# Loading weight pieces three items ahead, and splitting the rounding from the subtraction

## The chip, the cores and the metric

The kernel runs on one core of a Trainium2 chip. The metric is the device time of one execution in microseconds (us), from three runs. The engines are named as the profile names them: PE multiplies matrices, ACT is the scalar engine, DVE the vector engine, POOL the GpSimd engine, and SP issues most of the transfers. Each works through its own instructions in order and waits for the others by semaphores.

## The reference

An attention is followed by two feed-forward layers, and all data are float32.

```python
scores = q @ k.T / 8 + bias          # 4 batches x 8 heads, 576 x 576, D = 64
x = softmax(scores) @ v              # -> 2304 tokens x 512
h = x @ w_in                         # 512 -> 2048
x = (h * clip(h + 3, 0, 6) / 6) @ w_out
e = argmax(x @ w_gate)               # 8 experts, one for each token
out = gate * relu(x @ w1[e]) @ w2[e]
```

The change touches the conversion of `w_in` and `w_out` alone. They come as 64-bit floats, in 32 pieces of 128 x 512 numbers.

## The kernel before

**Attention.** The work is cut into 80 items (a chunk of rows, a unit of four heads, a pair of heads). In the loop over `s`, one pass does the scores of item `s`, the exponentials and sums of item `s-1`, the transposes of item `s-3` and the product with V of item `s-4`. The string `ORDER = "T0 S T1 X0 X1 Q0 Q1 P N"` sets the order within a pass: `S` is the place of the side work, between the two halves of the transposes (T0, T1). A transposed half is copied out of PSUM by ACT and by DVE.

**Side work.** `Moe.early` hangs steps on passes. Pieces 0 to 3 of the weights are converted there, in passes from 36 on, eight passes apart. The load brings the piece as pairs of 32-bit words into the tile `wraw` (512 KB, issued on SP). Then follow `s_a` (ACT, scales the upper word, L611), `s_b` (DVE, shift, L614), `s_c` (DVE, two steps, L617 and L618: the float32 value is then in `t[1]`), and `s_d`: ACT rounds that to the high part (L621) and DVE subtracts the high part from the value and gets the low part (L622). The last two belong to one step.

**First feed-forward layer.** It works in blocks of 256 tokens. A unit is one block and 128 of the 2048 inner features: `l1_` has 12 matmuls with 256 columns (L679), ACT adds and cuts (`r`, L685), DVE makes `t` (L686), ACT the high part of `g` (L688), DVE the low part (L691); `l2_`, three units behind, has 6 matmuls with 512 columns (L709). The first three blocks run interleaved over 48 units, numbered `g` = 0 to 47 here. Pieces 4 to 31 are converted meanwhile: `tick(p)` gives four functions, of which `l1_` calls the first after `t`, the second and third after the high `g`; the fourth comes after the low `g`. Two of three units have a tick: 28 in all.

The results of L679 go to four PSUM banks in turn. When the third block's accumulators are made, in `l2_` with `b == 2`, they take two of the four for good, so from there a result of L679 has two banks, each free again when DVE has made its `t`.

Of the kernel before, what the change touches and what calls it, by code (L numbers as in the profile page):

```python
# [6 lines left out]
F32 = mybir.dt.float32  # L7
# [4 lines left out]
ALU = mybir.AluOpType  # L12
# [3 lines left out]
B, H, S, D = 4, 8, 576, 64  # L16
# [502 lines left out]
class Moe(Base):  # L519
# [83 lines left out]
    def w_steps(self, p, t):  # L603

        nc = self.nc
        raw = self.raws.pop(p)
        w = self.pieces[p] = self.w_piece(p)
        a, b = t[0], t[1].bitcast(I32)

        def s_a():  # L610
            nc.scalar.activation(a, raw[:, :, 1].bitcast(F32), AF.Copy, scale=2.0 ** -112)  # L611

        def s_b():
            nc.vector.tensor_scalar(b, a.bitcast(I32), 3, None, op0=ALU.logical_shift_left)  # L614

        def s_c():
            nc.vector.scalar_tensor_tensor(b, raw[:, :, 0], 29, b, op0=ALU.logical_shift_right, op1=ALU.bitwise_or)  # L617
            nc.vector.scalar_tensor_tensor(b, a.bitcast(I32), -2147483648, b, op0=ALU.bitwise_and, op1=ALU.bitwise_or)  # L618

        def s_d(lo):  # L620
            nc.scalar.copy(w[:, 0:512], t[1])  # L621
            lo.tensor_tensor(w[:, 512:], t[1], w[:, 0:512].bitcast(F32), op=ALU.subtract)  # L622

        return s_a, s_b, s_c, s_d

    def w_early(self, p):

        nc = self.nc
        S = {}

        def load():
            self.w_load(p, "cv" if p % 2 else "V2")

        def first():
            t = [self.tl("bt0", [512], name="cva"), self.tl("bt1", [512], name="cvb")]
            S["f"] = self.w_steps(p, t)
            S["f"][0]()

        return [load, first, lambda: S["f"][1](), lambda: S["f"][2](), lambda: S["f"][3](nc.vector)]


    def x_load(self, b):
# [518 lines left out]
            self.conv[p][2]()  # L1161
            self.w_loads(p + (3 if p < 6 else 4))

    def w_d(self, p):
        self.conv.pop(p)[3](self.nc.vector)

    def tick(self, p):
        return (lambda: self.w_b(p + 1), lambda: self.w_d(p), lambda: self.w_a(p + 2), lambda: self.w_c(p + 1)) if p < 32 else ()

    def early(self, N):  # L1170

        ex = {}
        add = lambda s, f: ex.setdefault(s, []).append(f)
        self.loaded, self.conv = 4, {}
        add(31, self.setup)
        add(34, self.setup2)
        for p in range(4):
            for k, f in enumerate(self.w_early(p)):
                add(36 + 8 * p + k, f)
        gen = self.emit()  # L1180
        self.first = gen
        add(73, lambda: [self.x_load(b) for b in range(3)])
        add(N - 3, lambda: self.w_loads(6))
        add(N - 1, lambda: self.w_a(4))
        add(N, lambda: (self.x_prep(0), self.w_b(4)))
        add(N + 1, lambda: (self.w_c(4), next(gen)))
        add(N + 2, lambda: (self.x_prep(1), next(gen)))
        return ex
# [200 lines left out]
```

## Time and profile before

| what | value |
|---|---|
| median of 3 runs | 1071.23 us (1069.64 to 1074.22) |
| profiled execution, its own time | 1073.36 us |
| its span, first to last instruction | 1071.6 us |
| attention passes with side work of this kind | about 209 to 311 us of the span |
| 48 interleaved units | about 360 to 511 us of the span |

The profiled execution has its time 1.8 us above its span, and stands 2.1 us above the median. An engine's busy share says little here; what counts is, stage by stage, which wait PE sees.

### The profile page before, as it was taken

To read this page: it belongs to the slowest core of one execution; us is meant where nothing else is said; L and a number is where in the kernel's file an instruction comes from. 1 tells how busy PE (TensorE), PEld (TensorE's weight loads), DVE (VectorE), ACT (ScalarE), POOL (GpSimd) and SP (SyncE) were. 2 spreads that over 40 slices of the span, in tenths; PEclk is the share of its full clock that TensorE was granted. 3 is DMA by queue.
4 is the path that set the end of the run, shared out by engine and by line. 5 is a ranking of instruction groups with operands and counts; after the bars stand their busy time and mean duration, and the time that the engine had idled before them with its cause. 6 is when DMAs were issued, how large, how long until landed. Compare 5 with 4: busy or idle time off the path is not lost. (4 is left out here: it accounts for less than half of the span.)

```text
span 1071.6 us, 22490 instructions
## 1 busy us (share of the span) xinstructions
PE 1014.0 (95%) x8373; PEld 799.7 (75%) x8373; DVE 620.8 (58%) x1578; ACT 539.5 (50%) x1222; POOL 220.6 (21%) x273
## 2 busy tenths in 40 slices
PE   5898999989999989999999999999999989999996
PEld 2355556767777779988888889888887868777774
DVE  4886886768887767775445343436464633355310
ACT  4677788767778745554333333333352233354421
POOL 0132233534454200000010000002212242221111
PEclk9999999989999989999999999999999989999998
DMA  7564582423234134440202011010502185786850
GB/s 243 177 195 154 176 270 75 116 75 100 78 101 119 58 120 128 127 135 3 72 9 40 1 40 41 1 40 1 201 17 50 53 272 189 270 288 259 329 171 32
DMA packets 62198, 129.29 MB, mean 121 GB/s; under 512 B 13820, under 2 KB 35708, under 8 KB 59264
## 3 DMA queue, kind: packets, MB, share of 16 engines
q1 hardware_dynamic: 57424, 117.69, 33.3%
q0 software_dynamic: 4512, 9.49, 3.0%
q8 instruction: 68, 1.11, 0.4%
q10 hardware_dynamic: 144, 0.59, 0.2%
q14 instruction: 50, 0.41, 0.1%
HBM read 164.08 MB, written 14.65 MB: 167 GB/s over the span
## 5 line engine op out<-in xcount | busy, mean ns | idle before, releaser
L709 PE MATMUL acc<-wp,g 128*128 128x512 f32 x864 | 225.3, 396 | 0.7 <-DVE t L686 0.6
L679 PE MATMUL ph<-xh,wp 128*128 128x256 f32 x1024 | 207.0, 285 | 2.5 <-DVE eT L368 1.3
L679 PEld LDWEIGHTS ph<-xh,wp 128*128 128x128 f32 x1024 | 166.3, 189 | 12.2 <-issue 3.9
L709 PEld LDWEIGHTS acc<-wp,g 128*128 128x128 f32 x864 | 153.1, 189 | 27.5 <-DVE t L686 1.2
L344 POOL TENSOR_SCALAR e<-e,st 128x576 f32<-128x576 f32 (+1 forms) x160 | 126.2, 800 | 229.5 <-DVE st L342 109.2
L679 PE MATMUL ph<-xl,wp 128*128 128x256 f32 x512 | 144.2, 282 | 0.4 <-issue 0.4
L327 DVE CUSTOM_DVE_ANT_0 e<-sc,bias 128x576 f32<-128x576 f32 (+1 forms) x160 | 116.0, 752 | 46.4 <-PE sc L324 42.6
L685 ACT ACTIVATE r<-ph,small 128x256 f32<-128x256 f32 x144 | 67.5, 468 | 124.1 <-PE ph L679 119.0
L335 ACT ACTIVATE e<-e,st 128x576 f32<-128x576 f32 (+1 forms) x160 | 123.0, 774 | 0.0
L686 DVE SCALAR_TENSOR_TENSOR t<-r,ph 128x256 f32<-128x256 f32 x144 | 60.3, 419 | 107.8 <-ACT r L685 98.8
L688 ACT ACTIVATE g<-t 128x256 fp32r<-128x256 f32 x144 | 60.2, 418 | 114.2 <-DVE t L686 113.2
L1032 PE MATMUL peh<-ws,xt 128*128 128x512 f32 x408 | 102.8, 406 | 4.1 <-PEq L1341 4.0
L324 PE MATMUL sc<-K,q 64*128 64x288 f32 (+1 forms) x640 | 104.6, 426 | 0.4 <-DVE st L327 0.4
L679 PEld LDWEIGHTS ph<-xl,wp 128*128 128x128 f32 x512 | 96.7, 189 | 3.4
L783 POOL DMA_INDIRECT tab_d<-small x18 | 18.2, 1009 | 380.1 <-DVE small L781 343.0
L691 DVE SCALAR_TENSOR_TENSOR g<-t,g 128x256 fp32r<-128x256 f32 x144 | 61.0, 424 | 56.2 <-ACT g L688 55.7
L1032 PEld LDWEIGHTS peh<-ws,xt 128*128 128x128 f32 x408 | 76.9, 192 | 22.2 <-issue 4.9
L378 PE MATMUL po<-eT,V 128*64 128x128 f32 (+1 forms) x1280 | 82.2, 271 | 4.2 <-ACT eT L366 2.4
L1060 PE MATMUL peo<-ws,ehh 128*128 128x512 f32 x272 | 86.2, 398 | 0.0
L362 PEld LDWEIGHTS pt<-cst,e 64*128 64x128 f32 x1296 | 60.3, 139 | 34.5 <-issue 10.4
L378 PEld LDWEIGHTS po<-eT,V 128*64 128x64 f32 x1280 | 64.3, 138 | 27.4 <-issue 14.7
L362 PE MATMUL pt<-cst,e 64*128 64x64 f32 x1296 | 72.6, 232 | 8.6 <-ACT eT L366 3.5
(215 smaller groups left out, 1453.4 us busy)
## 6 DMA issues: line engine op xcount, KB each, us to landing
er<-in_we SPq DMA_DIRECT2D x46, 1024.0 KB
er<-in_we SPq DMA_DIRECT2D x86, 512.0 KB
xb<-in_xb SPq DMA_DIRECT2D x38, 512.0 KB
wraw<-in_wf SPq DMA_DIRECT2D x32, 512.0 KB
cv<-in_xb SPq DMA_DIRECT2D x11, 512.0 KB
K<-in_kT SPq DMA_DIRECT2D x8, 576.0 KB
xr<-xT_d SPq DMA_DIRECT2D x9, 512.0 KB
y_d<-y SPq DMA_DIRECT2D x18, 256.0 KB
```

Source lines behind the costliest of these rows:

```text
L324: nc.tensor.matmul(self.sc[i][:R, n, :288], q[d, pr, :], self.kv[u][d, pr, n * 288:(n + 1) * 288], start=True, stop=True, tile_position=(6 ...
L327: nc.vector.tensor_tensor_reduce(out=e[:R, j, :].rearrange("p (n s) -> p n s", n=2), in0=self.sc[j][:R, :, :288], in1=self.bias[c][:R, 4 * ...
L335: self.nc.scalar.activation(e[:R, j, :], e[:R, j, :], AF.Exp, scale=-1.0, bias=st[:R, j:j + 1], accum_out=st[:R, 4 + j:5 + j])
L344: nc.gpsimd.tensor_scalar(e[:R, j, :], e[:R, j, :], st[:R, 6 + j:7 + j], 1.0, op0=ALU.mult, op1=ALU.mult)
L362: nc.tensor.transpose(pts[h][:, i - a, :], src[i][d], self.ident[d, d], tile_position=(64 * h, 0))
L378: nc.tensor.matmul(po[64 * j:64 * j + 64, :], vm[:, 2 * pr + j, kb, :], eT[:, 2 * kb + j, :], start=kb == 0, stop=False, tile_position=(0, ...
L679: nc.tensor.matmul(ph, w, x[c], start=n == 0, stop=n == 11)
L685: nc.scalar.activation(r, ph, AF.Relu, bias=self.three)
L691: nc.vector.scalar_tensor_tensor(g[:, 1], t, 1.0 / 6.0, g[:, 0].bitcast(F32), op0=ALU.mult, op1=ALU.subtract)
L709: nc.tensor.matmul(acc[t], x, w, start=f == 0 and i == 0, stop=f == 15 and i == 2)
L1032: nc.tensor.matmul(ph[:, n, :], a, w, start=c == 0 and i == 0, stop=c == 3 and i == 2)
L1060: nc.tensor.matmul(d["po"], a, w, start=f == 0 and i == 0, stop=f == 7 and i == 2)
```

## The change

The step `s_d` becomes two, `s_d` (ACT's rounding) and `s_e` (DVE's subtraction). In the attention a piece is loaded at pass 34 + 8p instead of 36 + 8p, `s_a` stays at 37 + 8p, `s_b` at 38 + 8p, `s_c` at 39 + 8p, the rounding at 40 + 8p, and the subtraction goes to 41 + 8p. In a tick the rounding moves ahead of the shift of the next piece, into the first of the four functions; the subtraction stays in the second.

```diff
-        def s_d(lo):
+        def s_d():
             nc.scalar.copy(w[:, 0:512], t[1])
-            lo.tensor_tensor(w[:, 512:], t[1], w[:, 0:512].bitcast(F32), op=ALU.subtract)
-
-        return s_a, s_b, s_c, s_d
+
+        def s_e():
+            nc.vector.tensor_tensor(w[:, 512:], t[1], w[:, 0:512].bitcast(F32), op=ALU.subtract)
+
+        return s_a, s_b, s_c, s_d, s_e
...
-        return [load, first, lambda: S["f"][1](), lambda: S["f"][2](), lambda: S["f"][3](nc.vector)]
+        return [load, first] + [lambda k=k: S["f"][k]() for k in range(1, 5)]
...
-    def w_d(self, p):
-        self.conv.pop(p)[3](self.nc.vector)
-
     def tick(self, p):
-        return (lambda: self.w_b(p + 1), lambda: self.w_d(p), lambda: self.w_a(p + 2), lambda: self.w_c(p + 1)) if p < 32 else ()
+
+        return (lambda: (self.conv[p][3](), self.w_b(p + 1)), lambda: self.conv.pop(p)[4](), lambda: self.w_a(p + 2),
+                lambda: self.w_c(p + 1)) if p < 32 else ()
...
         for p in range(4):
-            for k, f in enumerate(self.w_early(p)):
-                add(36 + 8 * p + k, f)
+            for k, f in zip((34, 37, 38, 39, 40, 41), self.w_early(p)):
+                add(8 * p + k, f)
```

The first place is SP's queue around piece 0, where `wraw` is the piece's tile and `xT_d` the attention's result. Before:

```order
L388 DMA xT_d<-xo_580_2657 128x2x128
L305 DMA q_2769<-in_qT 128x2x64
L388 DMA xT_d<-xo_598_2746 128x2x64
L291 DMA V_615_2827<-in_vM 128x1024
L293 DMA VT_616_2828<-in_vT 64x2x64 x2
L584 DMA wraw_2833<-in_wf 128x1024
L305 DMA q_2891<-in_qT 128x2x128
```

And now:

```order
L388 DMA xT_d<-xo_580_2657 128x2x128
L584 DMA wraw_2719<-in_wf 128x1024
L305 DMA q_2771<-in_qT 128x2x64
L388 DMA xT_d<-xo_599_2748 128x2x64
L291 DMA V_616_2829<-in_vM 128x1024
L293 DMA VT_617_2830<-in_vT 64x2x64 x2
L305 DMA q_2891<-in_qT 128x2x128
```

The load of the piece has moved ahead of one load of q, one store of the result and the three loads of a V tile.

The second place is ACT's queue in the first ticks of the feed-forward layer. Before:

```order
L611 ACTIVATE cvc_5496<-wraw_5138 128x512
L685 ACTIVATE r_5512<-ph_5499,small_562_2558 128x256
L688 ACTIVATE g_5514<-t_5513 128x256
L621 CAST wp_5254<-cvb_5253 128x512
L611 ACTIVATE cva_5521<-wraw_5363 128x512
L685 ACTIVATE r_5543<-ph_5530,small_562_2558 128x256
L688 ACTIVATE g_5545<-t_5544 128x256
L621 CAST wp_5254<-cvd_5497 128x512
```

And now:

```order
L611 ACTIVATE cvc_5496<-wraw_5138 128x512
L687 ACTIVATE r_5512<-ph_5499,small_562_2558 128x256
L621 CAST wp_5254<-cvb_5253 128x512
L690 ACTIVATE g_5514<-t_5513 128x256
L611 ACTIVATE cva_5521<-wraw_5363 128x512
L687 ACTIVATE r_5543<-ph_5530,small_562_2558 128x256
L621 CAST wp_5254<-cvd_5497 128x512
L690 ACTIVATE g_5545<-t_5544 128x256
```

The rounding (CAST) now stands between `r` and the high `g`; DVE's queue is the same in the ticks, and in the attention its four subtractions stand one pass later.

## Rows read from the trace of the kernel before

**Rows 1.** The page: span, and PE's granted clock in 40 slices.

```profile
span 1071.6 us, 22490 instructions
...
PEclk9999999989999989999999999999999989999998
```

**Rows 2.** Timeline of ACT: start, duration, instruction, idle before it and its releaser.

```profile
216.90 0.66 ACT L611 ACTIVATE cva<-wraw 128x512 f32<-128x512 f32 x1 [4.24 <-DMA wraw<-in_wf]
...
245.22 0.73 ACT L611 ACTIVATE cva<-wraw 128x512 f32<-128x512 f32 x1 [1.13 <-DMA wraw<-in_wf]
...
272.77 0.70 ACT L611 ACTIVATE cva<-wraw 128x512 f32<-128x512 f32 x1 [0.75 <-DMA wraw<-in_wf]
...
299.30 0.70 ACT L611 ACTIVATE cva<-wraw 128x512 f32<-128x512 f32 x1 [0.99 <-DMA wraw<-in_wf]
...
379.59 0.67 ACT L611 ACTIVATE cvc<-wraw 128x512 f32<-128x512 f32 x1 [1.93 <-DMA wraw<-in_wf]
```

**Rows 3.** Timeline of SP: the issue of the fourth early load.

```profile
294.95 0.42 SPq L584 DMA_DIRECT2D wraw<-in_wf  x1
```

**Rows 4.** Timeline of PE behind the first early load.

```profile
217.87 0.79 PE L362 MATMUL pt<-cst,e 64*128 64x64 f32 x10 [2.88 <-ACT eT L366]
```

**Rows 5.** Windows, attention passes: window and length, busy by engine (count), PEclk, DMA share, GB/s.

```profile
212.30:225.21 12.91, 9.14 (x100) 7.08 (x97) 5.77 (x18) 5.43 (x15) 4.08 (x6) 0.74 0.32 87
347.76:353.95 6.19, 6.19 (x99) 5.08 (x96) 4.94 (x17) 4.96 (x15) 2.93 (x4) 1.00 0.35 130
243.70:248.12 4.42, 3.27 (x54) 2.40 (x51) 3.02 (x13) 3.29 (x9) 1.47 (x2) 1.00 0.27 95
341.81:344.66 2.85, 2.85 (x52) 2.25 (x50) 2.76 (x11) 2.39 (x8) 1.46 (x2) 1.00 0.00 0
...
298.10:302.23 4.13, 3.18 (x50) 2.23 (x48) 2.40 (x9) 3.14 (x9) 1.46 (x2) 1.00 0.63 187
330.28:333.32 3.04, 3.04 (x50) 2.22 (x48) 2.27 (x9) 2.33 (x8) 1.47 (x2) 1.00 0.02 5
```

**Rows 6.** Timeline of DVE, units 6 and 7 of the first feed-forward layer.

```profile
385.61 0.42 DVE L686 SCALAR_TENSOR_TENSOR t<-r,ph 128x256 f32<-128x256 f32 x1
...
387.02 0.69 DVE L622 TENSOR_TENSOR wp<-cvd,wp 128x512 fp32r<-128x512 f32 x1 [0.65 <-ACT wp L621]
...
389.29 0.41 DVE L686 SCALAR_TENSOR_TENSOR t<-r,ph 128x256 f32<-128x256 f32 x1
```

**Rows 7.** Timeline of PE, `l2_` of unit 4 and what follows.

```profile
384.82 0.96 PE L709 MATMUL acc<-wp,g 128*128 128x512 f32 x3 [0.28 <-DVE t L686]
386.08 0.96 PE L709 MATMUL acc<-wp,g 128*128 128x512 f32 x3 [0.30 <-DVE t L686]
389.76 2.93 PE L679 MATMUL ph<-wp,wp 128*128 128x256 f32 x12 [2.71 <-DVE t L686]
392.49 2.76 PE L709 MATMUL acc<-wp,g 128*128 128x512 f32 x6
395.05 0.41 PE L679 MATMUL ph<-xh,wp 128*128 128x256 f32 x1
```

**Rows 8.** Windows, columns as in 5: three places where PE had been idle.

```profile
34.30:42.70 8.40, 6.80 (x44) 2.83 (x45) 7.68 (x17) 5.30 (x10) 2.22 (x4) 1.00 0.59 209
79.06:84.80 5.74, 3.06 (x14) 1.06 (x14) 2.40 (x4) 3.85 (x8) 1.46 (x2) 0.70 0.09 22
384.40:395.41 11.01, 7.71 (x28) 6.04 (x27) 7.64 (x17) 5.04 (x11) 0.00 (x0) 0.69 0.48 144
```

**Rows 9.** Windows, columns as in 5: 12 units and the 24 behind them.

```profile
398.02:431.66 33.64, 33.64 (x217) 30.53 (x216) 26.17 (x55) 17.90 (x40) 0.00 (x0) 1.00 0.38 113
431.66:500.09 68.43, 68.43 (x434) 60.84 (x432) 50.75 (x107) 34.98 (x78) 0.00 (x0) 1.00 0.32 99
```

**Rows 10.** Timeline: DVE's low `g` of a unit, and PE's `l2_` of that unit.

```profile
420.35 0.42 DVE L691 SCALAR_TENSOR_TENSOR g<-t,g 128x256 fp32r<-128x256 f32 x1
...
424.67 1.54 PE L709 MATMUL acc<-wp,g 128*128 128x512 f32 x6
```

## The prediction

> **What bounds the kernel now.** I read the page first: PE's clock stays near full but for four slices of 40 [rows 1], so the time is PE's own work plus the places where it waits. Then I looked up who waits for the loads and roundings that the change moves, and what PE does in that moment.
>
> In the attention ACT stands still before four of the conversion's first steps until the piece has landed: 4.24, 1.13, 0.75 and 0.99 us [rows 2]. Behind ACT in its queue stand the copies of transposed halves, and PE waits for those: 2.88 us behind the first [rows 4]. The reader should see in the windows what that costs. The two passes around the first load take 12.91 us, with 100 matmul rows; two passes of the same shape without side work take 6.19 us for 99, and the clock in the long window is 0.74, in the short 1.00 [rows 5]. A pass with the second load's wait takes 4.42 us against 2.85, one with the fourth's 4.13 against 3.04 [rows 5].
>
> In the feed-forward layer a second cause shows. In a tick, DVE waits 0.65 us for ACT's rounding before it subtracts [rows 6], since ACT rounds only after the high `g`, and that waits for `t`. While DVE is behind, a tick therefore lasts from one `t` at 385.61 to the next at 389.29, 3.68 us [rows 6]; PE's work for a unit is 33.64 / 12 = 2.80 us [rows 9]. At units 4 to 8 DVE is behind, and PE falls from four result banks to two: it idles 0.28 + 0.30 + 2.71 = 3.29 us for `t` [rows 7], and the next pair of `l1_` and `l2_` then runs at a mean clock of 0.69 over that window [rows 8].
>
> **Load three passes ahead.** The fourth load was issued at 294.95 and used at 299.30 after its wait, so it landed within 4.35 us [rows 2, 3]. Three passes are about 3 x 6.19 / 2 = 9.3 us [rows 5]. All four waits should go. In SP's queue only a store stands where the first load now goes, and its tile was read last in pass 33; behind it wait q, which is loaded two chunks early, and V, four passes early.
>
> *First load.* The excess is 12.91 - 6.19 = 6.72 us. Some of it is the work of `s_a` and `s_b`, which stays; an ACT step is 0.66 us [rows 2]. So 5.7 (6.72 less an ACT step, and a bit for DVE) to 6.7; I take 6.2, since the step fits into ACT's idle time as often as not.
>
> *The other three.* Excess 4.42 - 2.85 = 1.57 and 4.13 - 3.04 = 1.09, together 2.66 with nothing for the third. If ACT's own steps of 0.73 and 0.70 [rows 2] are what costs in these passes, 1.2 is left; the waits themselves sum to 2.87. I take 2.2.
>
> **Subtraction a pass later, in the attention.** It does the same DVE work between the same neighbours, and the rounding that it needs is a pass old. The trace of before does not price it in the new place. Its bound is a wait like the 0.65 us in [rows 6] times four, either way; I take nothing, because DVE has other work in the pass before the subtraction and PE would notice neither.
>
> **Rounding ahead in the ticks.** ACT's order becomes `r`, rounding, high `g`. The value to round was finished in the tick before, so the rounding runs while DVE makes `t` and shifts the next piece. DVE's 0.65 us falls away, and a lagging tick goes from 3.68 to about 3.0 us.
>
> *Units 4 to 8.* Four subtractions lie ahead of the `t` at 389.29. Two of their savings run into ACT's wait of 1.93 us for a landing at 379.59 [rows 2]. That load is released by a DVE step and starts only one saving earlier, so of the first two 0.65 us comes through. Then two more: 3 x 0.65 = 2.0 us. PE's idle time there falls from 3.29 to about 1.3 us, 1.7 if the parts overlap badly. The pair after it took 395.05 - 389.76 = 5.29 us [rows 7] where 2.80 is normal, so 2.5 us more come back if the clock stays up. Between the ends 2.0 and 4.5 I decide by the nearest rows. After an idle time of 8.40 - 6.80 = 1.60 us the clock stayed at 1.00; after 5.74 - 3.06 = 2.68 us the window's mean was 0.70 [rows 8]. 1.3 to 1.7 us is nearer the first. I take 4.5 us.
>
> *The later ticks.* There DVE is just too slow for PE: 24 units take 68.43 us, where 24 x 2.803 = 67.27 is PE's own pace [rows 9]. All of 1.15 us should come back, at worst none of it. I take 1.1.
>
> **Sum.** 6.2 + 2.2 + 4.5 + 1.1 = 14.0 us. The profiled execution took 1073.36 us, so 1059.4 by its own time; it stands 2.1 us above the median of 1071.23, and off that the forecast is 1057.2 us. No term moves a transfer of the later layers against the work it feeds, so nothing in the rows takes the gain back.
>
> **The rivals.**
>
> *The clock falls all the same at unit 8.* If the idle time is enough for it, 2.5 us of the third term stay lost: 11.5 us saved, 1059.7. For it: in the window of [rows 8] that ends at 395.41 PE had been idle in pieces before the clock fell, and the remaining idle time lies between the two other rows. Against it: the nearer row kept its clock. The Trainium skill, in "TensorE: Matmul & The Clock Gate", Part 1 on the clock gate, says that the slow clock is the default and that PE's activity is what releases it. By that rule what counts is how busy PE was, not one gap's length, which would bring this rival about; the trace agrees in that the windows of its idle times of 2.68 us and more have a low mean clock.
>
> *The attention is held by something else.* With ACT's wait gone, its steps and DVE's shifts, still in the same passes, might cost PE half of what it lost. Then the first two terms give 4.2 in place of 8.4 us: 1061.4. For it: DVE is busy 2.40 us in the 4.42 us window and ACT 3.29 [rows 5], so a pass of 2.85 us would be tight for ACT. Against it: ACT's busy time in the unloaded pass of 2.85 us is already 2.39, and its 0.7 us more still leaves room over two passes.
>
> *The load doesn't come forward.* If SP were held at the new place, by the release of the tile or by the store ahead of it, the piece would land no sooner. The first two terms are lost and 5.6 us stay: 1065.6. Against it: the order shows one store ahead of the load and no wait for side work.
>
> *Slower: the high `g` comes late.* Rounding stands ahead of it now. If `l2_` waited for `g`, each of 28 ticks would put the rounding, 0.65 us by the wait that it caused [rows 6], on PE's path: 18 us, so 1071.2 - 8.4 + 18.2 = 1081.0 with the attention's gain kept. It decides from the point at which the low `g` has less room than that ahead of PE. Against it: a low `g` that ends at 420.35 + 0.42 = 420.77 is first read by matmuls starting at 424.67, 3.9 us later [rows 10].
>
> **How the numbers follow.** The forecast has 0.55, the fallen clock 0.25, the half gain in the attention 0.11, the load that does not come 0.05, the late `g` 0.02; 0.02 is left for a chance that I don't see. A measurement of this kernel can tell about 0.5%, 5.4 us, from no change. All cases but the last three, and half of the load's, end clearly below 1065.8: faster 0.94, same 0.04, slower 0.02. The smallest sum is 5.7 + 1.2 + 2.0 + 0 = 8.9 us, 1062.3; the largest 6.7 + 2.7 + 4.5 + 1.2 = 15.1, 1056.1. The three runs of before spread over 4.6 us, so I widen by about one on either side: 1054.5 to 1063.5.
>
> **What would show it right or wrong.** ACT should have no wait for `wraw` in passes 37 to 61, and the two passes at the first load should take 6.2 to 7.2 us at a clock of 1.00. The wait of DVE for the rounding should be gone from the ticks and the 24 units should take 67.3 us. The idle time of PE before unit 8 should be below 1.7 us, and the slice that holds it should show a clock of 9. The prediction is wrong if PE waits at the same passes for DVE or for another ACT step, if the clock falls somewhere else, or if PE waits for a high `g`.

## The result, and the profile after

| kernel | median of runs | range |
|---|---|---|
| before | 1071.58 us (4 runs) | 1069.64 to 1074.22 |
| changed | 1058.45 us (4 runs) | 1057.27 to 1060.79 |

The ratio of the runs is 0.986, with a 95% interval of 0.9835 to 0.9886: faster by 1.1 to 1.7%. By the medians it is 13.1 us; 14.0 were forecast. The profiled execution of the changed kernel took 1060.79 us and is the slowest of its four.

The page of the changed kernel, its span and the clock in 40 slices, beside [rows 1]:

```profile
span 1059.0 us, 22473 instructions
...
PEclk9999999999999999999999999999999989999998
```

The two 8s in slices 9 and 15 are gone: those of the first early load and of unit 8. What remains late in the run was there before. Two short falls of the clock in the attention are too small for a slice to show; the account of the prediction takes them up.

The first steps of the conversion, by the view of the tile `wraw` in the changed kernel, what its readers waited for (us, times):

```profile
its engine sat idle before it (us, times) until:
  DMA wraw<-in_wf: 2.1, 1
```

Five waits stood there [rows 2]; the four in the attention are gone, and the fifth, in the feed-forward layer, is not shorter. The same passes as in [rows 5] in windows of the changed kernel, from pass 37, 45 and 61 on:

```profile
214.82:221.10 6.28, 6.28 (x99) 5.07 (x97) 5.62 (x18) 5.48 (x16) 3.10 (x4) 1.00 0.38 108
240.22:243.36 3.14, 3.06 (x54) 2.33 (x51) 3.02 (x13) 3.14 (x9) 1.48 (x2) 1.00 0.00 0
294.00:297.04 3.04, 3.04 (x50) 2.22 (x47) 2.27 (x9) 2.81 (x9) 1.47 (x2) 1.00 0.20 81
```

12.91 us have become 6.28, 4.42 have become 3.14, and 4.13 have become 3.04, at a clock of 1.00. In the third window ACT's extra step costs nothing at all: the unloaded pass takes 3.04 us too [rows 5].

In the feed-forward layer, DVE's timeline of the changed kernel around the tick that [rows 6] shows:

```profile
378.94 0.42 DVE L688 SCALAR_TENSOR_TENSOR t<-r,ph 128x256 f32<-128x256 f32 x1
379.28 0.42 DVE L614 TENSOR_SCALAR cvb<-cva 128x512 int32<-128x512 int32 x1
379.61 0.68 DVE L624 TENSOR_TENSOR wp<-cvd,wp 128x512 fp32r<-128x512 f32 x1
...
381.88 0.41 DVE L688 SCALAR_TENSOR_TENSOR t<-r,ph 128x256 f32<-128x256 f32 x1
```

The subtraction follows the shift with no wait, and from one `t` to the next the tick takes 2.94 us, not 3.68. PE's timeline there, beside [rows 7]:

```profile
379.38 1.53 PE L711 MATMUL acc<-wp,g 128*128 128x512 f32 x6
382.35 1.68 PE L681 MATMUL ph<-wp,wp 128*128 128x256 f32 x12 [1.44 <-DVE t L688]
383.87 0.39 PE L711 MATMUL acc<-wp,g 128*128 128x512 f32 x1
```

The three waits of 3.29 us in all are one of 1.44 us, and the granted clock behind it is 1.00. In windows of the changed kernel, units 7 to 9 and then the 12 and the 24 units of [rows 9]:

```profile
377.97:388.06 10.09, 8.65 (x55) 7.54 (x54) 7.85 (x18) 6.16 (x14) 0.00 (x0) 1.00 0.54 158
388.06:421.76 33.70, 33.70 (x218) 30.57 (x216) 26.93 (x57) 19.36 (x41) 0.00 (x0) 1.00 0.40 125
421.76:489.52 67.76, 67.76 (x434) 61.23 (x432) 49.73 (x105) 36.47 (x76) 0.00 (x0) 1.00 0.30 94
```

For the kernel before, units 7 to 9 in one window:

```profile
382.96:398.02 15.06, 11.76 (x56) 9.75 (x54) 9.68 (x21) 5.71 (x14) 0.00 (x0) 0.77 0.35 106
```

So 15.06 us have become 10.09, and the 24 units take 0.67 us less.

### The profile page after: what moved, and what is told of

Read it like the earlier page. It is cut to its first block, busy times and chain, and to the rows that moved or that the text cites. A ratio compares the mean times of both kernels' runs of the same rounds, so it can differ in the third digit from the quotient of the medians.

```text
span 1059.0 us, 22473 instructions
## 1 busy us (share of the span) xinstructions
PE 1010.0 (95%) x8373; PEld 797.4 (75%) x8373; DVE 620.1 (59%) x1578; ACT 544.1 (51%) x1222; POOL 221.2 (21%) x273
## 5 line engine op out<-in xcount | busy, mean ns | idle before, releaser
L324 PEld LDWEIGHTS sc<-K,q 64*128 64x128 f32 (+1 forms) x640 | 60.3, 178 | 23.9 <-issue 11.2
```

Source lines behind the costliest of these rows:

```text
L324: nc.tensor.matmul(self.sc[i][:R, n, :288], q[d, pr, :], self.kv[u][d, pr, n * 288:(n + 1) * 288], start=True, stop=True, tile_position=(6 ...
```

## The experiments

My theory was that two parts act, each in a place of its own: the earlier loads in the attention, and the rounding ahead of the high `g` in the ticks, while the later subtraction does nothing. The main rivals were that the later subtraction frees the attention, and that the layer's gain is only a matter of where the clock fell. Four kernels take the change apart.

**The loads alone.**

```diff
-                add(36 + 8 * p + k, f)
+                add((36 if k else 34) + 8 * p + k, f)
```

> The kernel before, with the four loads in the attention two passes earlier (34 + 8p) and nothing else. My theory: all four waits of ACT for wraw go, the two passes at the first load take 6.2 to 6.8 us instead of 12.9, and the run is 8 to 9 us faster than before; the idle time of PE at unit 8 of the feed-forward layer stays at about 2.7 us. Rival, the later subtraction is what frees the attention: the run is less than 3 us faster.

Measured: a ratio of 0.9924 to before (0.9899 to 0.9949), 8.2 us by the ratio. No wait for `wraw` in the attention; the passes at the first load take what they take in the changed kernel. Units 7 to 9 keep their trouble, PE's wait of 2.7 us for `t` with them, as this window shows:

```profile
377.00:390.66 13.66, 10.64 (x56) 8.82 (x55) 9.17 (x20) 5.69 (x13) 0.00 (x0) 0.88 0.36 117
```

**The ticks alone.** The changed kernel with the attention's steps back in their passes:

```diff
-            for k, f in zip((34, 37, 38, 39, 40, 41), self.w_early(p)):
+            for k, f in zip((36, 37, 38, 39, 40, 40), self.w_early(p)):
```

> The change with the attention's steps put back to their old passes (load at 36 + 8p, rounding and subtraction both at 40 + 8p): only the order in the ticks is new. My theory: DVE's wait for the rounding goes, PE's idle time before unit 8 is 1.3 to 1.7 us and the clock stays up behind it, 5 to 6 us faster than before. Rival, the feed-forward layer gained only since the earlier stage ended elsewhere in time and the clock happened not to fall: no more than 2.5 us faster, with a fallen clock at unit 8.

Measured: 0.9961 (0.9942 to 0.9981), 4.2 us by the ratio, which is a little under the expectation and above the rival's 2.5; the interval, 2.0 to 6.2 us, holds both. The trace decides, and has the theory's places: units 7 to 9 in 9.95 us at a clock of 1.00, and 67.76 us for the 24 units:

```profile
381.87:391.82 9.95, 8.66 (x55) 7.53 (x54) 7.73 (x17) 6.17 (x14) 0.00 (x0) 1.00 0.48 158
425.52:493.28 67.76, 67.76 (x434) 61.23 (x432) 49.73 (x105) 36.46 (x76) 0.00 (x0) 1.00 0.29 94
```

These are the changed kernel's numbers, though the layer's first matmul came at 359.4 us, close to the 360.5 of before and not at the changed kernel's 355.5. The rival falls.

**The later subtraction alone.** Loads at 36 + 8p and the old ticks, with the subtraction at 41 + 8p:

```diff
+            for k, f in zip((36, 37, 38, 39, 40, 41), self.w_early(p)):
...
+        def both():
+            f = self.conv.pop(p)
+            f[3]()
+            f[4]()
+
+        return (lambda: self.w_b(p + 1), both, lambda: self.w_a(p + 2), lambda: self.w_c(p + 1)) if p < 32 else ()
```

> The kernel before, with the subtraction of pieces 0 to 3 one pass later than the rounding; loads and ticks as before. My theory: nothing, within 1 us of before, and the four waits of ACT stay at 4.2, 1.1, 0.8 and 1.0 us. Rival, the later subtraction is what frees the attention: 5 us or more faster.

Measured: 0.9986 (0.9968 to 1.0005), which contains no change; the waits for `wraw` stay. The rival of 5 us is out. But the stages say that it is not nothing either. Here are their lengths in us, from the first score matmul of one pass to that of another, each kernel with its one trace. The stretches named are those with side work of the kind; the changed kernel is its run of the second comparison, below.

| passes | before | loads alone | subtraction alone | changed |
|---|---|---|---|---|
| 37 to 39 | 16.14 | 10.01 | 16.11 | 10.00 |
| 40 to 44 | 15.27 | 15.63 | 15.04 | 15.39 |
| 45 to 49 | 18.63 | 17.33 | 18.24 | 16.99 |
| 53 to 57 | 17.11 | 17.04 | 16.96 | 16.69 |
| 61 to 65 | 16.27 | 15.32 | 15.76 | 15.01 |
| 66 | 3.30 | 3.30 | 3.61 | 3.60 |
| sum | 86.72 | 78.63 | 85.72 | 77.68 |

The loads give 8.1 us, and the later subtraction 0.9 to 1.0 us, with the loads or without. It comes from the first three pieces: the pass behind each old place, 41, 49 and 57, gets shorter by 0.25, 0.35 and 0.36 us. With the fourth piece pass 64 gains 0.46 us, and passes 65 and 66 lose as much. Timelines of POOL and DVE around the first and the fourth subtraction, of the kernel before:

```profile
229.17 0.74 POOL L344 TENSOR_SCALAR e<-e,st 128x576 f32<-128x576 f32 x1 [3.48 <-ACT wp L621]
229.28 1.17 DVE L622 TENSOR_TENSOR wp<-cvb,wp 128x512 fp32r<-128x512 f32 x1
...
309.17 1.25 POOL L344 TENSOR_SCALAR e<-e,st 128x576 f32<-128x576 f32 x1 [1.55 <-ACT wp L621]
309.20 0.69 DVE L622 TENSOR_TENSOR wp<-cvb,wp 128x512 fp32r<-128x512 f32 x1 [0.22 <-ACT wp L621]
```

And of the changed kernel:

```profile
228.27 0.75 POOL L344 TENSOR_SCALAR e<-e,st 128x576 f32<-128x576 f32 x1 [0.88 <-ACT xo L386]
228.87 0.69 DVE L624 TENSOR_TENSOR wp<-cvb,wp 128x512 fp32r<-128x512 f32 x1
...
306.52 0.75 POOL L344 TENSOR_SCALAR e<-e,st 128x576 f32<-128x576 f32 x1 [0.94 <-PE pt L362]
306.63 1.17 DVE L624 TENSOR_TENSOR wp<-cvb,wp 128x512 fp32r<-128x512 f32 x1
```

In the old place three of four subtractions began 0.11 us behind a step of POOL's normalising and took 1.17 us. The fourth began 0.03 us behind one and took 0.69; there POOL's step took 1.25 us in place of 0.74. In the new place two begin 0.6 us behind POOL's step and one finds POOL idle: 0.68 to 0.71 us. The fourth, 0.11 us behind a step, takes 1.17. That is 3 - 1 = 2 times 0.48, about 1.0 us of DVE's time.

The Trainium skill, in "SBUF — State Buffer", on SBUF's two separate sides, says that GpSimd and a DVE step with two SBUF inputs share a port as an exclusive lock, which goes to whoever starts first. The trace agrees: with POOL 0.11 to 0.60 us ahead, the subtraction ended 0.54 us after POOL's step, whenever it had begun (230.45 after 229.91, and 229.56 after 229.02). Only at 0.03 us was it POOL that waited, though the profile has it first.

So the change did not move the subtractions out of POOL's way, but to places where three of them wait less for it and the fourth more. That three passes gain by this is argued from the durations. For the fourth the experiment that gives it to POOL, below, shows what the longer subtraction costs.

**The other bank for unit 8.** Is it DVE's lag or the hand-over of the banks that costs PE its idle time? When two of the four banks go to the third block's accumulators, unit 8 got the one that unit 7 had used. The kernel before, with the other order:

```diff
-            own, Base.banks = sorted(Base.banks)[:2], sorted(Base.banks)[2:]
+            own, Base.banks = sorted(Base.banks)[:2], sorted(Base.banks)[:1:-1]
```

> The kernel before, with the two result banks that are left after the third block's accumulators taken in the other order, so that unit 8 gets the bank of unit 4, whose t is long done, instead of unit 7's. My theory of unit 8: its wait of 2.71 us for t and the fallen clock behind it both go, 4 to 5 us faster than before, though DVE is as late as before. Rival, it is DVE's lag as such that costs: PE waits the same time one unit later, at most 1 us faster.

Measured: 0.9979 (0.9957 to 1.0001), 2.3 us by the ratio and not sure to be a gain. Windows of that kernel, for units 7 to 9, the 12 units and the 24:

```profile
387.34:397.50 10.16, 9.26 (x55) 7.33 (x53) 8.20 (x17) 4.54 (x11) 0.00 (x0) 1.00 0.36 108
397.50:432.02 34.52, 34.52 (x216) 30.22 (x216) 27.05 (x56) 18.03 (x41) 0.00 (x0) 1.00 0.39 122
432.02:501.00 68.98, 68.98 (x434) 60.70 (x434) 50.87 (x107) 35.56 (x79) 0.00 (x0) 1.00 0.31 100
```

At the place itself the theory holds: 15.06 us become 10.16, with the clock at 1.00. But 34.52 - 33.64 = 0.9 us and 68.98 - 68.43 = 0.6 us are given back, as DVE is still too slow for PE and its lag now reaches PE in the ticks that follow (with the quicker ticks, below, it does not). So 3.4 us are left, between theory and rival. The two other traces with the old ticks and banks took 13.66 and 13.79 us for units 7 to 9; against these 2.0 to 2.1 us are left, near the 2.3 of the whole time. The trace with the other bank order also has a fallen clock in the attention, in passes 45 to 49 (20.00 us against 18.63), ahead of the place that the edit touches.

A second comparison, on another chip, has the changed kernel as its own baseline.

> The changed kernel once more, on the same chip as the three runs beside it, as their baseline: 1.1 to 1.5% faster than before, as in the result; with the sum of the two parts' own gains (0.76% for the loads, 0.39% for the ticks) 1.15% if they simply add up.

Measured: 0.9888 (0.9863 to 0.9913), median 1063.65 us against 1075.93. The parts alone make 0.9924 x 0.9961 = 0.9885: they add up.

**The changed kernel with the other bank order** (the same line as above).

> The changed kernel with the bank order of the earlier experiment. My theory: units 7 to 9 take 8.4 us in place of 10.1, and as DVE now is fast enough in the ticks, nothing is given back in the 36 units behind: 1.3 to 1.7 us faster than the changed kernel. Rival, the lag of DVE comes back to PE later as it did without the change: the 36 units take 1 us more and the run is no faster than the changed kernel.

Measured: 0.9862 (0.9838 to 0.9886), median 1061.60 us. Units 7 to 9 take 8.40 us, which is three times PE's pace, and nothing is given back:

```profile
378.36:386.76 8.40, 8.40 (x56) 7.62 (x55) 7.34 (x17) 5.54 (x13) 0.00 (x0) 1.00 0.50 154
386.76:420.45 33.69, 33.69 (x217) 30.57 (x216) 27.32 (x58) 19.69 (x42) 0.00 (x0) 1.00 0.43 134
420.45:488.21 67.76, 67.76 (x433) 61.24 (x432) 49.77 (x105) 36.47 (x76) 0.00 (x0) 1.00 0.31 94
```

The rival falls: with the rounding ahead, DVE keeps up. In the stages that is 10.25 - 8.40 = 1.85 us of the baseline; the two intervals overlap, so the whole time does not separate the two kernels.

**Two passes ahead, not three.**

```diff
-            for k, f in zip((34, 37, 38, 39, 40, 41), self.w_early(p)):
+            for k, f in zip((35, 37, 38, 39, 40, 41), self.w_early(p)):
```

> The changed kernel with the loads at 35 + 8p, two passes ahead of the first step instead of three. My theory: a load needs at most 4.4 us and two passes are 6.2, so no wait of ACT for wraw in the attention and the same time as the changed kernel within 0.3%. Rival, the third pass is needed, as transfers ahead of it in the queue hold it up: waits of ACT of 1 us or more come back, 1 to 3 us slower than the changed kernel.

Measured: 0.9893 (0.9869 to 0.9918), as the baseline's 0.9888. No wait for `wraw` in the attention, and all five stages of the table within 0.02 us of the changed kernel's. The third pass is reserve.

**The subtraction on POOL in the attention.**

```diff
-            nc.vector.tensor_tensor(w[:, 512:], t[1], w[:, 0:512].bitcast(F32), op=ALU.subtract)
+            (nc.gpsimd if p < 4 else nc.vector).tensor_tensor(w[:, 512:], t[1], w[:, 0:512].bitcast(F32), op=ALU.subtract)
```

> The changed kernel with the four subtractions of the attention on POOL instead of DVE. Theory: what is left of the side work's price in the attention is DVE's time; taking 0.7 to 1.2 us of it per piece away from DVE saves 0.3 to 0.7 us per piece, 1 to 3 us in all. Rival: POOL's normalising gets late behind it and PE waits for POOL, no gain or up to 3 us slower.

Measured: 0.9854 (0.983 to 0.9878), its median 2.7 us under the baseline's; the two intervals overlap. The stages show less: 15.39, 17.00, 16.68 and 14.80 us behind pass 40, against 15.39, 16.99, 16.69 and 15.01. Three pieces gain nothing. The fourth gains 0.21 us in pass 65 and 0.26 in pass 66, of which 0.2 is lost again before the layer's first matmul. DVE was freed with all four (13.65 against 14.28 us in the mean of those stages), but PE noticed only the subtraction that took 1.17 us: 0.21 + 0.26 = 0.47 us, what it had lost by POOL. My theory holds for that piece and falls for the other three, whose 0.68 to 0.71 us of DVE cost PE nothing. The rest of the side work's price stays open. It shows in the passes of `s_c` and the ones behind, with the first three pieces: 3.73 and 3.86 us for passes 39 and 40, where passes 67 to 78 take 2.6 to 3.2.

**Both additions**, beside the changed kernel once more.

> The changed kernel as the baseline of the run beside it: 1.1 to 1.4% faster than before.

> The changed kernel with the other order of the two banks and with the four subtractions of the attention on POOL. From the stages of the two single runs: 1.7 us from units 7 to 9 and about 0.5 us from the passes behind the fourth piece, so 2 us faster than the changed kernel in the stages, 1.3 to 1.6% faster than before. Rival: the two were noise, and the run is the changed kernel's within 0.5 us in those stages.

Measured: the changed kernel 0.9854 (0.9827 to 0.988), median 1059.93 us, a little more gain than expected; with both additions 0.9848 (0.9823 to 0.9873), 1057.07. Units 7 to 9 take 8.39 us in place of 10.04, and passes 61 to 78 take 54.40 in place of 54.88. That is 2.1 us in the stages, which the whole time can't tell from nothing. It has the lowest ratio here, and beats the kernel before clearly, the changed one by its stages alone.

## Why the prediction was right, point by point

**The clock's four low slices and the waits as the bound** was right: two of the four slices went with the waits.

**Load three passes ahead.** Taken at 6.2 + 2.2 = 8.4 us; the loads alone give 8.1 in the stages and 8.2 by the ratio. The first is worth 5.8 of them, 6.1 up to pass 39 less 0.4 in pass 40, and the others 2.3. The rival by which the attention would be held by something else (4.2 us) did not come, nor the load that fails to come forward; it would be in time even with two passes.

**Subtraction a pass later** was taken at nothing, with a bound of four times 0.65 us. This term was mis-sized: it gives 0.9 to 1.0 us, inside the bound. The reason that I gave for nothing, that PE would notice neither place, was wrong: PE noticed where the subtraction waits for POOL. I had looked at what the step does, and not at what POOL does at that moment.

**Units 4 to 8.** Taken at 4.5 us with the clock up. The idle time left was 1.44 us where I had 1.3 to 1.7, the clock stayed, and the stage gave 15.06 - 10.09 = 4.97. The rival of the fallen clock did not come in any of the eight traces with the new ticks, two of which have no idle time there. But the profile of before was not typical in the size: the two other kernels with the old ticks and banks took 13.66 and 13.79 us there, with a mean clock of 0.88 in both against 0.77. Against these the stage gains 3.6 to 3.7 us, which is what the ticks alone show by the ratio (4.2, with the next term). The choice between the ends went by the length of one idle time; it came out right, but that length does not decide alone, as the last section shows.

**The later ticks.** Taken at 1.1 us, measured 0.67. PE's weight loads waited 1.6 us for `t` there before, and nothing of PE waits now; it takes 67.76 / 24 = 2.82 us per unit. The pace of 2.80 that I took from the 12 units ahead is simply not that of the 24 behind.

**The late high `g`.** No wait of PE for `g` shows in the changed kernel. What took the place of DVE's wait is harmless: over the 36 units behind unit 9 DVE waited 15.5 us for the rounding before. The view of the waits, DVE alone, of the kernel before (total us, times, longest) has

```profile
DVE wp L622 <- ACT wp L621: 15.5, 23, 1.0
```

and that of the changed kernel, with no row for the rounding,

```profile
DVE t L688 <- ACT r L687: 15.4, 13, 1.5
DVE g L693 <- ACT g L690: 6.3, 13, 0.5
```

DVE now waits for `r`, and `r` for PE (31.3 us over the same units).

**The clock somewhere else.** I had named this as a sign of being wrong, and the trace of the changed kernel shows it in two places. In pass 20, ahead of all side work of this kind, the clock fell after PE had been idle for 1.77 us, where PE was idle 1.1 to 1.5 us in the other traces; the pass took 8.74 us, and 6.45 to 6.90 elsewhere. The other place is passes 55 and 56, in the last section. Neither came back in the changed kernel's two other traces, so they are not counted against a term. Whether the new order makes the second likelier is not settled: two of eight traces with the early loads have it, none of four without.

**The sum.** By stages the change gives 9.0 us in the attention, 3.5 to 5.0 at units 7 to 9 and 0.6 behind them: 13.1 to 14.6 us. The whole times gave 13.1, 12.3 and 14.1 us by medians in three comparisons. That the forecast of 14.0 lies so near is in part luck: against the traces with the higher clock the third term is 0.9 too large and the fourth 0.4, and the later subtraction, taken at nothing, brings 1.0. The rest of the execution differs by more than these from trace to trace: from the first expert's first matmul to the end the changed kernel took 282.31, 283.56 and 285.27 us in its three traces.

## What to carry to other kernels

Where an engine that others wait for takes work from a transfer, count the transfer's landing in passes of the loop and issue it that much ahead: here at most 4.4 us of landing against passes of 3.1, so two passes; a third brought nothing more. A step whose result another engine needs belongs where its own engine would wait anyway. Here the rounding went into the time in which ACT had waited for `t`; DVE's 15.5 us of waits for it went, and PE got no wait in their place. Removing one stall shows whether the engine behind it keeps up: with the slow DVE loop, the better bank order gave back 1.5 of the 3.5 to 4.9 us that it had won, and with the quick one nothing. A step that is moved should be looked at beside what the other engines do at its new place, and the stage be followed until its passes are equal again: pass 66 took back what pass 64 had won.

## What the runs showed of the hardware that was not expected

The clock fell in the attention with no idle time of PE over 0.41 us just ahead of it, in two of the eight traces with the early loads. Here are the stretch before it, in a window of the changed kernel, and the same stretch of the passes in its second trace, where the clock stayed:

```profile
274.15:277.59 3.44, 2.62 (x29) 1.72 (x26) 3.41 (x10) 2.62 (x7) 0.74 (x2) 1.00 0.51 117
```

```profile
273.82:277.26 3.44, 2.62 (x29) 1.72 (x26) 3.40 (x10) 2.62 (x7) 0.74 (x2) 1.00 0.50 110
```

PE was busy 2.62 of 3.44 us in both, with the same three idle times of 0.20, 0.41 and 0.21 us. In the first trace the granted clock then went to 0.5, the 1.2 GHz level; passes 53 to 57 took 18.14 us there and 16.69 in the other, so 1.45 us. It came and went between executions of the same kernel. The Trainium skill's "TensorE: Matmul & The Clock Gate", Part 1, says that the clock is set by how busy PE has been. The trace agrees in that no single long idle time was needed; why the same work had two outcomes, no run here shows. A fallen clock in one profile is thus not yet a term: it, and its length, have to be seen in more than one.
